# A transform and two gated layers on one core: another order at the transform's beginning, and a second engine for the copies of high halves

## The chip, the cores and the metric

The kernel runs on one core of one Trainium2 chip. The metric is device time in microseconds (us), lower is better: 1006.93 us is the median of three runs of the kernel before (1006.16 to 1008.03).

TensorE (PE) multiplies, VectorE (DVE), ScalarE (ACT) and GpSimd (POOL) do the elementwise work, and SyncE (SP) issues most DMAs. ScalarE issues a few DMAs at the start, and GpSimd issues one in each step of the first layer. Each engine works through its own list of instructions in order and waits on semaphores for the others.

## The reference

```python
def _attn_ref(x):                      # x: (2, 3008, 256)
    X = np.fft.fft(x, axis=1)
    X = np.fft.fft(X, axis=2)
    return X.real.astype(np.float32)
def _moe_ref(x, w_gate, w_val, w_out): # x: (6016, 256), 256 -> 1536 -> 256
    gate = 1.0 / (1.0 + np.exp(-(x @ w_gate)))
    val = x @ w_val
    return (gate * val @ w_out).astype(np.float32)
def _moe2_ref(x, w_in, w_out):         # 256 -> 2048 -> 256
    h = x @ w_in
    g = h * np.cos(h)
    return (g @ w_out).astype(np.float32)
def reference(**kwargs):
    ...
    x = attn_out.reshape(B * S, D)
    x = _moe_ref(x=x, **moe_kwargs)
    return _moe2_ref(x=x, **moe2_kwargs)
```

The weights reach the chip as float64 numbers (the kernel reads their bits), x as float32. The kernel computes in float32.

## The kernel before

**Transform.** A sequence of 3008 = 64 x 47 is transformed in three stages of matmuls. In the first, 16 chunks (c = 0 to 15) of 8 columns each are multiplied with the 47-point table: the columns of x are the stationary operand, and each chunk fills two banks of PSUM (the tile `ps`), which ScalarE or VectorE copies to the tile `D1`. x comes in 256 KB pieces: `load_x2` (line 421) fetches two chunks with three DMAs into one of three buffers `raws`, in turn. Chunks 0 and 1 lie in `raws[0]` and have DMAs of their own; `raws[1]` holds chunks 2 and 3, `raws[2]` chunks 4 and 5, then `raws[0]` again 6 and 7, and so on. A buffer is loaded anew when TensorE has left it. The loads write 96 of 128 partitions, so each buffer is zeroed once before its first load. Behind chunk `CX0` four small matmuls on the tile `xs` (line 476) make a correction that ScalarE and VectorE add to `D1`. The second stage (`stage_b`, table `T1`) has 12 groups, the third (`stage_c` and `c_piece`, table `T3`) 6 blocks of tokens; it leaves the tokens' even and odd parts in `eo`. Part of the third stage is done between the first steps of the next layer.

**First layer.** 72 steps s, each one tile of 128 of the 1536 hidden units f for one of six blocks of 502 token pairs t (table `TF`; the first 12 steps take f = 0 to 5 for t = 0 and 1, the next 12 take f = 6 to 11). In a step TensorE makes two pairs of products (`ab(s, 0)` into banks 4 and 5, `ab(s, 1)` into banks 6 and 7). VectorE joins them (`even`, lines 645 to 647, then `tokens`, line 653). ScalarE takes the sigmoid (line 815), GpSimd multiplies gate and value (`times`, line 657), ScalarE splits the product into a high part and a negated one (`hi1`, lines 755 and 756), and GpSimd issues a DMA that adds the product to the latter (`lo1`, line 693), which leaves the low part. Four steps later TensorE multiplies with the output weights (`out1(s - 4)`, lines 670 to 673). All matmuls are done on split values: high times high, low times high, high times low. The second layer has the same form with a cosine and starts when the first has ended.

**Weights.** They arrive as float64 bits, and the chip turns them into float32. A unit of 128 x 512 numbers goes through `dec_steps`: scale (ScalarE, line 170), sign (line 145 or 146), size (line 151 or 153), clamp (VectorE, line 157), shift (VectorE, line 162), add (GpSimd, line 167); for the first layer's input weights a difference and a sum (lines 231 and 232); and then the split, `hilo_steps`: a copy to the high half and a subtraction for the low one.

```python
        def high():
            at[:] = views()
            A.copy(at[0], src())
        ...
        return [(A, .63, high), (VG, {V: 1.1, G: 1.3}, low)]
```

A unit stands in a slot `u0` to `u17`: the input weights of tile f in `u0` to `u11`, the output weights of tiles 2k and 2k + 1 in the slot numbered 12 + k. So `u15` holds the output weights of tiles 6 and 7, and `out1(12)`, the first product of tile 6, needs it in step 16.

**What sets the order.** The engines' lists are fixed when the program is built. A planner keeps a clock for each engine (`clk`), adds estimated times to them, and puts steps of the weights' decoding between the regular work wherever an engine's clock leaves room (`fill`, line 318); `may` (line 256) says which engine takes a step that two can do, and `need` (line 352) finishes a unit at the place where it is first used. While the transform runs, the low half goes to whichever of VectorE and GpSimd would end it first; once the first layer has begun (`begun`) all low halves go to GpSimd. Small changes of the estimates or of the order of loads move many instructions. The constants `cmax`, `czero` and `cone`, which the decoding on VectorE reads, lie at the end of PSUM bank 7, the bank of the second product of `ab(s, 1)`.

**The beginning**, lines 427 to 447:

```python
        for r in raws[1:]:
            G.memset(r, 0.0)
        ...
        A.dma_start(out=xs[0:96], in_=x0)
        clk[DQ] = 4.3
        for p in range(1, NX2):
            load_x2(p)
            if p == 1:
                fill(DQ, clk[DQ] + 1.7)
```

Of the kernel before, what the change touches and what calls it, by code (L numbers as in the profile page):

```python
# [34 lines left out]
JC = 8  # L35
# [1 line left out]
JH = 3  # L37
NX2 = 3
NWARM = 7
CX0 = 4  # L40
L1, L2 = 4, 5

INV2PI = float(np.float32(1 / (2 * np.pi)))
# [12 lines left out]
def fft_moe_moe(ctx: ExitStack, tc: tile.TileContext, x, x0, head, w1, w1s, wo1, w2, t1, t3, out):  # L56
# [19 lines left out]
    ps = pp.tile([128, 8, 512], F32, name="ps")  # L76
# [47 lines left out]

    DQ = nc.sync
    clk = {V: 0.0, A: 0.0, G: 0.0, DQ: 0.0}
    VG, VA = (V, G), (A, V)
    begun = [False]

    def spend(e, us, after=0.0):  # L130
# [47 lines left out]
    def hilo_steps(views, src):  # L178
        at = []

        def high():
            at[:] = views()
            A.copy(at[0], src())

        def low(e):
            e.tensor_tensor(out=at[1], in0=src(), in1=f32(at[0]), op=ALU.subtract)

        return [(A, .63, high), (VG, {V: 1.1, G: 1.3}, low)]

    ws = [dpool.tile([128, 2 * UC], F32, name=f"ws{u}") for u in range(NF2)]  # L190

# [59 lines left out]
    beside = [0.0]  # L251

    def cost(step, e):
        return (step[1][e] if step[0] in (VG, VA) else step[1]) + (beside[0] if e is V else 0)

    def may(un, e):

        step = un[2][0]
        if step[0] not in (VG, VA):
            return e is step[0]  # L260
        if e not in step[0] or begun[0] and step[0] is VG and e is V:
            return False
        if begun[0] and step[0] is VG:
            return True
        other = step[0][1 - step[0].index(e)]
        mine, theirs = (max(un[3], clk[q]) + step[1][q] for q in (e, other))
        return mine <= theirs + (VLATE if e is V else 0)
# [6 lines left out]
    def step_of(un, e=None):  # L274
        if len(un[2][0]) > 3 and not un[1]:
            at = max(un[3], clk[un[2][0][0]])
            while not (room_at(at, True) or free):
                finish(next(o for o in live if o[1] and o[0][0] in DIRECT))
            bf = room_at(at) or room_at(at, True) or free[0]
            free.remove(bf)  # L280
            un[1].append(bf)
            un[4].append(bf[0])
            un[3] = max(un[3], bf[2])
        step = un[2].pop(0)
        if step[0] in (VG, VA):
            e = e or (G if begun[0] and step[0] is VG else min(step[0], key=lambda q: max(clk[q], un[3]) + step[1][q]))
            step[2](e)
        else:
            e = step[0]
            step[2]()  # L290
        un[3] = spend(e, cost(step, e), un[3]) + (3.3 if e is DQ else .15)
        if not un[2]:
            live.remove(un)
            free.extend([buf, end, un[3], of] for buf, end, _, of in un[1])
# [23 lines left out]
    def fill(e, until):  # L318

        while True:  # L320
            begin(until)
            for un in live:
                step = un[2][0]
                if may(un, e):
                    at = max(un[3], clk[e])
                    if len(step) > 3 and not un[1] and not room_at(at):
                        continue
                    if at + cost(step, e) <= until:
                        step_of(un, e)
                        break  # L330
            else:
                if e is DQ and clk[e] + 1.5 <= until:
                    if queued:
                        load_next()
                        continue
                    if len(todo) > held[0] and todo[0][0] == "w2":
                        ready = [p for p in pairs() if max(bf[2] for bf in p) <= until]
                        if ready:
                            start(ready[0])
                            continue  # L340
                return
# [69 lines left out]
    with tc.tile_pool(name="xp", bufs=1) as xp:  # L411

        raws = [xp.tile([128, 2 * JC, 2, 64], F32, name=f"raw{i}") for i in range(NX2)]

        def rows(e, out, src):
            for k in range(3):
                e.dma_start(out=out[k:128:4], in_=src[32 * k:32 * (k + 1)])

        def load_x2(p):

            raw, src = raws[p % NX2].rearrange("p (c j) s n -> p c j s n", c=2), x[:, 2 * p:2 * p + 2]
            rows(DQ, raw, src)
            spend(DQ, 2.2)

        DQ.dma_start(out=hd[0:96], in_=head)
        DQ.dma_start(out=raws[0][0:96, JH:JC], in_=x[:, 0, JH:JC])
        DQ.dma_start(out=raws[0][0:96, JC:2 * JC], in_=x[:, 1])
        G.memset(warm, 0.0)  # L430
        for c_, k_ in ((cmax, FMAX), (czero, 0.0), (ps[:, 7, 509:510], 1.0)):
            V.memset(c_, k_)
        V.memset(hd2, 0.0)
        V.memset(hd[96:128], 0.0)
        V.memset(raws[0][96:128], 0.0)
        V.memset(raws[0][0:96, 0:JH], 0.0)
        for r in raws[1:]:
            G.memset(r, 0.0)
        V.memset(xs[96:128], 0.0)
        V.memset(halfpi, HALFPI)  # L440
        rows(A, hd2, head[:, 0:96])
        A.dma_start(out=xs[0:96], in_=x0)
        clk[DQ] = 4.3
        for p in range(1, NX2):
            load_x2(p)
            if p == 1:
                fill(DQ, clk[DQ] + 1.7)


        for _ in range(NWARM):  # L450
            PE.matmul(ps[:, 6, 0:128], warm, warm, start=True, stop=True)

        now = 3.5
        clk[V] = clk[G] = clk[A] = 4.5
        for c in range(NJC):
            if c == 10:
                DQ.dma_start(out=T1, in_=t1)
                DQ.dma_start(out=T3, in_=t3)
                spend(DQ, 1.4)
            ahead_a = AHA if c < NJC - 2 else (4, .4, 2, .5) if c < NJC - 1 else (4, .1, 2, -.8)  # L460
            nx = (c + 1) // 2 - 1 + NX2
            if nx < NJC // 2:

                ahead_a = (6.9 + (2 * nx - 1) * 1.79 + XLATE - 2.3 - 2.2 - now - 1.79,) + ahead_a[1:]
            slot(now, 1.79, ahead_a)
            b0 = 2 * (c % 3)
            for j in range(JC):
                q = ps[:, b0 + j // 4, (j % 4) * 96:(j % 4 + 1) * 96]
                if c == 0 and j < JH:
                    xj = hd[:, 96 + j * 128:96 + (j + 1) * 128]  # L470
                else:
                    xj = raws[c // 2 % NX2][:, c % 2 * JC + j].rearrange("p s n -> p (s n)")
                PE.matmul(q, xj, T2[c // 2 > 0], start=True, stop=True)  # L473
            if c == CX0:
                for i in range(2):
                    PE.matmul(ps[:, b0 + i, 384:480], xs[:, i], T2[0], start=True, stop=True)
            if c % 2 and c // 2 + NX2 < NJC // 2:
                clk[DQ] = max(clk[DQ], now + 1.79)
                load_x2(c // 2 + NX2)

            def evac(c=c, b0=b0, at=now + (1.79 if c else 3.4)):
                src = ps[:, b0:b0 + 2, 0:384].rearrange("p a (q c) -> p c a q", c=96)
                dst = D1[:, :, c * JC:(c + 1) * JC].rearrange("p c (a q) -> p c a q", a=2)
                if c < NJC - 1 and max(clk[V], at) + .4 < max(clk[A], at):
                    regular(V, .96, at)
                    V.tensor_copy(dst, src)
                elif c < NJC - 1:
                    regular(A, .8, at)
                    A.copy(dst, src)
                else:  # L490
                    regular(V, .5, at - .85)
                    V.tensor_copy(dst[:, :, 0], src[:, :, 0])
                    regular(A, .4, at)
                    A.copy(dst[:, :, 1], src[:, :, 1])
                if c == CX0:

                    A.mul(half, ps[:, b0, 384:480].rearrange("p (b s k) -> p b s k", b=B, s=2), .5)
                    f128 = ps[:, b0 + 1, 384:480].rearrange("p (b s k) -> p b s k", b=B, s=2)  # L500
                    d = D1[:, :, 0].rearrange("p (b s k) -> p b s k", b=B, s=2)
                    for r, sg in ((slice(0, 64), .5), (slice(64, 128), -.5)):
                        for cs in range(2):
                            V.scalar_tensor_tensor(
                                out=d[r, :, cs], in0=f128[r, :, 1 - cs], scalar=(sg if cs else -sg),
                                in1=half[r, :, cs], op0=ALU.mult, op1=ALU.add)
                    spend(A, .2)
                    spend(V, .5, clk[A])

            after.append(evac)  # L510
            now += 1.79 if c else 3.4
# [454 lines left out]
```

## Time and profile before

| | |
|---|---|
| median of three runs | 1006.93 us |
| the profiled execution: its time, its span | 1007.07 us, 1004.9 us |
| TensorE busy | 991.4 us (99%) |
| ScalarE, VectorE, GpSimd busy | 795.0, 747.4, 653.2 us |
| granted TensorE clock, mean | 0.999 |
| DMA rate in the first two of 40 slices of the span (50 us) | 302 and 332 GB/s |

The span runs from the first to the last instruction; the rest of an execution's time lies around it. TensorE is busy nearly all the time, so a stretch in which it waits is what the others can add or save. The profile counts the 99% over all stages: the first 36 us are the transform's first stage, the second and third end near 70 us, the first layer's steps run to about 480 us, and the second layer takes the rest.

### The profile page before, as it was taken

What the parts mean: (1) busy time and instruction counts of PE and PEld (TensorE: products, weight loads), DVE (VectorE), ACT (ScalarE), POOL (GpSimd) and SP (SyncE); (2) the same over time, 40 slices, a digit from 0 to 9 for tenths busy, and PEclk for the clock granted to TensorE, in tenths of its full rate; (3) what the DMA queues carried; (4) which work ended last, traced back from release to release, by engine and by line L of the source; (5) the groups of instructions that cost most, each with busy time, mean ns of one, the idle gap of its engine ahead of it and who ended that gap; (6) DMA issues with size and microseconds to landing.
All of it is one profiled execution on the core that took longest, in us unless ns stands there. A gap on an engine that the chain in (4) does not pass through costs nothing.

```text
span 1004.9 us, 13355 instructions
## 1 busy us (share of the span) xinstructions
PE 991.4 (99%) x4570; PEld 826.3 (82%) x4570; DVE 747.4 (74%) x1018; ACT 795.0 (79%) x1231; POOL 653.2 (65%) x521
## 2 busy tenths in 40 slices
PE   9999999999999999998999999999999999999998
PEld 8997888878888888787888888888888888888886
DVE  4898977887778777775777677777777777776775
ACT  5798767777777786856888888888988888888886
POOL 2678998888889898784445464554645455464643
PEclk9999999999999999999999999999999999999999
DMA  8804566678768768899000000000000000000000
GB/s 302 332 1 83 98 104 128 126 151 179 153 133 168 170 151 181 214 245 226 1 1 21 21 1 21 1 22 13 8 22 1 21 1 21 21 0 22 1 21 21
DMA packets 34644, 85.59 MB, mean 85 GB/s; under 512 B 3312, under 2 KB 25136, under 8 KB 33904
## 3 DMA queue, kind: packets, MB, share of 16 engines
q0 software_dynamic: 19584, 37.02, 21.4%
q1 hardware_dynamic: 14736, 47.59, 13.3%
q8 instruction: 36, 0.59, 0.3%
q14 instruction: 32, 0.26, 0.1%
q10 hardware_dynamic: 256, 0.14, 0.1%
HBM read 33.16 MB, written 14.56 MB: 47 GB/s over the span
## 4 chain that ended last, share of the span: by engine, by line
PE 90%; DMA 3%; DVE 3%; ACT 2%; issue 1%; POOL 1%; DVEq 0%; ACTq 0%; POOLq 0%; SPq 0%
PE ps L722 26%; PE ps L627 14%; PE ps L628 14%; PE ps L629 14%; PE ps L670 5%; PE ps L672 5%; PE ps L673 5%; PE ps L473 3%; DVE D L653 2%; DMA D<-D 2%; PE ps L569 1%; PE ps L529 1%; PE ps L530 1%; POOL D L657 1%; DMA ws<-D 1%
## 5 line engine op out<-in xcount | busy, mean ns | idle before, releaser
L748 POOL TENSOR_TENSOR D<-D,D 128x502 fp32r<-128x502 f32 x191 | 248.9, 1303 | 253.4 <-ACT D L747 239.1
L722 PE MATMUL ps<-D,u 128*128 128x502 f32 x1152 | 291.7, 389 | 0.0
L627 PE MATMUL ps<-es,u 128*128 128x502 f32 x672 | 262.9, 391 | 2.1 <-DVE D L653 1.2
L628 PE MATMUL ps<-es,u 128*128 128x502 f32 x672 | 262.3, 390 | 0.0
L629 PE MATMUL ps<-es,u 128*128 128x502 f32 x672 | 261.6, 389 | 0.0
L722 PEld LDWEIGHTS ps<-D,u 128*128 128x128 f32 x1152 | 216.7, 188 | 45.1
L657 POOL TENSOR_TENSOR D<-D 128x502 f32<-128x502 f32 x144 | 198.6, 1522 | 46.4 <-ACT D L815 46.1
L733 DVE SCALAR_TENSOR_TENSOR D<-D,ps 128x502 f32<-128x502 int32 x192 | 130.1, 678 | 122.0 <-POOL D L748 102.5
L653 DVE TENSOR_TENSOR D<-D,ps 128x1004 f32<-128x1004 f32 x144 | 172.9, 1201 | 49.5 <-PE ps L629 22.4
L732 ACT ACTIVATE D<-ps 128x502 int32<-128x502 f32 x192 | 113.1, 589 | 60.7 <-PE ps L629 58.1
L815 ACT ACTIVATE D<-D 128x1004 f32<-128x1004 f32 x72 | 75.0, 1041 | 97.1 <-DVE D L653 97.1
L627 PEld LDWEIGHTS ps<-es,u 128*128 128x128 f32 x672 | 126.5, 188 | 30.7 <-DVE D L653 2.3
L628 PEld LDWEIGHTS ps<-es,u 128*128 128x128 f32 x672 | 126.9, 189 | 25.9
L629 PEld LDWEIGHTS ps<-es,u 128*128 128x128 f32 x672 | 126.4, 188 | 26.4
L734 DVE SCALAR_TENSOR_TENSOR D<-D 128x502 f32<-128x502 int32 x192 | 142.3, 741 | 6.6
L740 DVE TENSOR_TENSOR D<-D,ps 128x502 f32<-128x502 f32 x192 | 128.8, 671 | 17.1 <-ACT D L739 17.1
L645 DVE SCALAR_TENSOR_TENSOR D<-eo,w,ps 128x502 f32<-128x502 f32 x144 | 101.4, 735 | 32.3 <-PE ps L629 31.9
L739 ACT ACTIVATE D<-D 128x502 f32<-128x502 f32 x192 | 120.0, 625 | 6.1
L738 ACT ACTIVATE D<-D 128x502 f32<-128x502 f32 x192 | 118.7, 618 | 4.3 <-DVE D L734 2.8
L747 ACT CAST D<-D 128x502 fp32r<-128x502 f32 x192 | 114.5, 596 | 0.3 <-DVE D L740 0.3
L672 PE MATMUL ps<-D,u 128*128 128x502 f32 x288 | 112.5, 391 | 1.2 <-ACT eo L689 1.2
L673 PE MATMUL ps<-D,u 128*128 128x502 f32 x288 | 111.9, 389 | 0.0
(95 smaller groups left out, 1103.8 us busy)
## 6 DMA issues: line engine op xcount, KB each, us to landing
D<-D POOLq DMA_DIRECT2D x72, 502.0 KB, 5.8
D<-in_w_dram SPq DMA_DIRECT2D x16, 512.0 KB, 4.9
ws<-D SPq DMA_DIRECT2D x16, 512.0 KB, 3.8
u<-ws SPq DMA_DIRECT2D x16, 512.0 KB, 5.4
u<-in_w_dram SPq DMA_DIRECT2D x12, 512.0 KB, 7.9
out_dram<-D SPq DMA_DIRECT2D x24, 251.0 KB, 2.7
raw<-in_x_dram SPq DMA_DIRECT2D x21, 256.0 KB, 5.1
u<-in_wo_dram SPq DMA_DIRECT2D x6, 512.0 KB, 7.7
```

Of the source, the lines that this page charges most:

```text
L627: PE.matmul(o, w_hi, m_hi, start=first, stop=False)
L628: PE.matmul(o, w_lo, m_hi, start=False, stop=False)
L629: PE.matmul(o, w_hi, m_lo, start=False, stop=last)
L653: V.tensor_tensor(out=gv[s][:, :, c:c + PC], in0=sas, in1=ps[:, 6:8, 0:PC], op=op)
L657: G.tensor_tensor(out=gv[p][:, 1, m], in0=gv[p][:, 1, m], in1=gv[p][:, 0, m], op=ALU.mult)
L672: PE.matmul(o, WO1(f)[:, 0, m], h[:, 0, sg], start=first, stop=False)
L673: PE.matmul(o, WO1(f)[:, 1, m], h[:, 0, sg], start=False, stop=False)
L722: PE.matmul(o, WO2(f)[:, i, d * 128:(d + 1) * 128], h[:, m], start=(f == 0 and i == m == 0), stop=(f == NF2 - 1 and m == 1))
L733: V.scalar_tensor_tensor(out=r, in0=k, scalar=-C1, in1=h, op0=ALU.mult, op1=ALU.add)
L734: V.scalar_tensor_tensor(out=r, in0=k, scalar=-C2, in1=r, op0=ALU.mult, op1=ALU.add)
L740: V.tensor_tensor(out=r, in0=r, in1=ps[:, 4 + s % 4, 0:PC], op=ALU.mult)
L748: (V if s == N2S - 1 else G).tensor_tensor(out=h[:, 1], in0=r, in1=f32(h[:, 0]), op=ALU.subtract)
```

## The change

The second buffer of x is zeroed in two halves, by GpSimd and VectorE, and it is the first thing VectorE does. The constants in PSUM come later. The load of `raws[2]` is issued right behind that of `raws[1]`, and the first weights (`fill(DQ, ...)`) follow both. The correction from `xs` moves from chunk 4 to chunk 6, and `xs`'s own DMA stands behind the loads in the text (ScalarE still issues it fourth). The copies to high halves may be taken by ScalarE or GpSimd during the transform; afterwards ScalarE has all of them, as before.

```diff
-CX0 = 4
+CX0 = 6
...
-        def high():
+        def high(e):
             at[:] = views()
-            A.copy(at[0], src())
+            if e is A:
+                A.copy(at[0], src())
+            else:
+                G.tensor_copy(at[0], src())
...
-        return [(A, .63, high), (VG, {V: 1.1, G: 1.3}, low)]
+        return [(AG, {A: .63, G: .8}, high), (VG, {V: 1.1, G: 1.3}, low)]
...
-        if e not in step[0] or begun[0] and step[0] is VG and e is V:
+        if e not in step[0]:
             return False
-        if begun[0] and step[0] is VG:
-            return True
+        if begun[0] and step[0] is not VA:
+            return e is (G if step[0] is VG else A)
...
-        for c_, k_ in ((cmax, FMAX), (czero, 0.0), (ps[:, 7, 509:510], 1.0)):
-            V.memset(c_, k_)
+        for e in (G, V):
+            r = raws[1].rearrange("p j s n -> p (j s n)")
+            e.memset(r[:, 0:JC * 128] if e is G else r[:, JC * 128:], 0.0)
         V.memset(hd2, 0.0)
         V.memset(hd[96:128], 0.0)
         V.memset(raws[0][96:128], 0.0)
         V.memset(raws[0][0:96, 0:JH], 0.0)
-        for r in raws[1:]:
+        for c_, k_ in ((cmax, FMAX), (czero, 0.0), (ps[:, 7, 509:510], 1.0)):
+            V.memset(c_, k_)
+        for r in raws[2:]:
             G.memset(r, 0.0)
...
-        A.dma_start(out=xs[0:96], in_=x0)
         clk[DQ] = 4.3
         for p in range(1, NX2):
             load_x2(p)
-            if p == 1:
-                fill(DQ, clk[DQ] + 1.7)
+        A.dma_start(out=xs[0:96], in_=x0)
+        fill(DQ, clk[DQ] + 1.7)
```

The changed program's line numbers are three to five higher (line 186 is 189, line 657 is 662).

SyncE's list at the beginning, before and then now (`raw1` and `raw2` are the buffers of x, `u0` and `u1` the first input weights, `eo0` here the room for the weights' odd row):

```order
L419 DMA raw1_115<-in_x_dram 32x2048 x3
L195 DMA eo0_82<-in_w1s_dram 128x48
L195 DMA u0_0_64<-in_w1_dram 128x1024
L419 DMA raw2_116<-in_x_dram 32x2048 x3
L195 DMA u1_0_65<-in_w1_dram 128x1024
```

```order
L422 DMA raw1_115<-in_x_dram 32x2048 x3
L422 DMA raw2_116<-in_x_dram 32x2048 x3
L198 DMA eo0_82<-in_w1s_dram 128x48
L198 DMA u0_0_64<-in_w1_dram 128x1024
L198 DMA u1_0_65<-in_w1_dram 128x1024
```

The second load of x now stands ahead of the first weights, and everything behind the fifth row is in the same order.

GpSimd's list in the first layer, from the product `times(11)` to `times(16)` before, then from `times(14)` to `times(16)` now (`D1` is the room for products and decoding, L657 or L662 is `times`, L693 or L698 the DMA of `lo1`, L186 or L189 a low half):

```order
L657 TENSOR_TENSOR D1_90<-D1_90 128x502 x2
L693 DMA D2_376<-D1_90 128x2x502
L186 TENSOR_TENSOR u11_1_1151<-D1_90,u11_1_1151 128x4x128
L186 TENSOR_TENSOR u15_1_1153<-D1_90,u15_1_1153 128x2x256
L657 TENSOR_TENSOR D1_90<-D1_90 128x502 x2
L693 DMA D2_376<-D1_90 128x2x502
L657 TENSOR_TENSOR D1_90<-D1_90 128x502 x2
L693 DMA D2_376<-D1_90 128x2x502
L167 TENSOR_TENSOR D1_90<-D1_90,u16_0_80 128x512
L167 TENSOR_TENSOR D1_90<-D1_90,u17_1_818 128x512
L657 TENSOR_TENSOR D1_90<-D1_90 128x502 x2
```

```order
L662 TENSOR_TENSOR D1_90<-D1_90 128x502 x2
L698 DMA D2_372<-D1_90 128x2x502
L167 TENSOR_TENSOR D1_90<-D1_90,u15_0_79 128x512
L167 TENSOR_TENSOR D1_90<-D1_90,u16_0_80 128x512
L662 TENSOR_TENSOR D1_90<-D1_90 128x502 x2
L698 DMA D2_372<-D1_90 128x2x502
L189 TENSOR_TENSOR u15_1_1295<-D1_90,u15_1_1295 128x2x256
L189 TENSOR_TENSOR u16_1_1297<-D1_90,u16_1_1297 128x2x256
L662 TENSOR_TENSOR D1_90<-D1_90 128x502 x2
```

The low half of `u15` stood behind `times(11)` and `lo1(10)`; it now stands behind `times(15)` and `lo1(14)`. The first rows of the two pieces are `times(11)` and `times(14)`.

VectorE's list between `tokens(4)` (first row) and `even(5)` (last row), before and then now (`u8`, `u9`, `u10` are units in decoding):

```order
L653 TENSOR_TENSOR D1_90<-D1_90,ps_63 128x2x502 x2
L162 SCALAR_TENSOR_TENSOR D1_90<-D1_90,ps_63 128x512
L157 SCALAR_TENSOR_TENSOR D1_90<-u10_0_74,ps_63 128x512
L645 SCALAR_TENSOR_TENSOR D1_90<-eo0_82,w128_88,ps_63 128x502 x2
L653 TENSOR_TENSOR D1_90<-D1_90,ps_63 128x2x502 x2
```

```order
L658 TENSOR_TENSOR D1_90<-D1_90,ps_63 128x2x502 x2
L157 SCALAR_TENSOR_TENSOR D1_90<-u8_0_72,ps_63 128x512
L162 SCALAR_TENSOR_TENSOR D1_90<-D1_90,ps_63 128x512
L157 SCALAR_TENSOR_TENSOR D1_90<-u9_0_73,ps_63 128x512
L650 SCALAR_TENSOR_TENSOR D1_90<-eo0_82,w128_88,ps_63 128x502 x2
```

Three steps of decoding stand there in place of two.

## Rows read from the trace of the kernel before

**Rows 1.** The page, busy time of each engine.
```profile
PE 991.4 (99%) x4570; PEld 826.3 (82%) x4570; DVE 747.4 (74%) x1018; ACT 795.0 (79%) x1231; POOL 653.2 (65%) x521
```

**Rows 2.** Waits of TensorE from 160 us on: us in total, times, longest.
```profile
PE ps L670 <- DMA D<-D: 2.5, 1, 2.5
PE ps L672 <- ACT eo L689: 1.2, 1, 1.2
PE ps L627 <- DVE D L157: 0.7, 1, 0.7
```

**Rows 3.** Timeline of TensorE, 1 to 16 us: start, us, what [idle before].
```profile
1.00 3.36 PE L451 MATMUL ps<-early 128*128 128x128 f32 x14 [1.00 <-POOL early L430]
4.15 1.43 PE L473 MATMUL ps<-early 128*128 128x96 f32 x6
5.38 3.46 PE L473 MATMUL ps<-early,raw 128*128 128x96 f32 x26
9.45 3.78 PE L473 MATMUL ps<-early,raw 128*128 128x96 f32 x32 [0.62 <-issue]
14.11 2.00 PE L473 MATMUL ps<-early,raw 128*128 128x96 f32 x16 [0.88 <-ACT D L489]
```

**Rows 4.** Timeline of SyncE's DMA queue, 0 to 20 us.
```profile
2.72 2.68 SPq L419 DMA_DIRECT2D raw<-in_x_dram  x3
...
6.70 2.15 SPq L419 DMA_DIRECT2D raw<-in_x_dram  x3
...
9.59 1.74 SPq L419 DMA_DIRECT2D raw<-in_x_dram  x3
...
13.27 1.75 SPq L419 DMA_DIRECT2D raw<-in_x_dram  x3
```

**Rows 5.** DMA issues, 9.5:11.36 and 13.2:15.1: KB each, median us to landing.
```profile
raw<-in_x_dram SPq DMA_DIRECT2D x3, 256.0 KB, 6.3
...
raw<-in_x_dram SPq DMA_DIRECT2D x3, 256.0 KB, 6.6
```

**Rows 6.** Timeline of GpSimd and of VectorE, 0 to 9 us, two memsets.
```profile
0.88 3.55 POOL L438 MEMSET raw<- 128x2048 f32 x2
...
4.19 0.38 DVE L436 MEMSET raw<- 96x384 f32 x1
```

**Rows 7.** Timelines of ScalarE, VectorE and TensorE, steps 1 and 5.
```profile
77.66 0.62 ACT L183 CAST u<-D 128x512 fp32r<-128x512 f32 x1
...
92.28 2.43 DVE L653 TENSOR_TENSOR D<-D,ps 128x1004 f32<-128x1004 f32 x2 [1.88 <-DMA D<-D]
94.63 0.68 DVE L162 SCALAR_TENSOR_TENSOR D<-D,ps 128x512 uint32<-128x512 uint32 x1
95.23 0.68 DVE L157 SCALAR_TENSOR_TENSOR D<-u,ps 128x512 f32<-128x512 f32 x1
...
95.96 0.49 PE L627 MATMUL ps<-es,u 128*128 128x502 f32 x1 [0.24 <-DVE D L157]
```

**Rows 8.** Timelines of ScalarE, GpSimd and TensorE, steps 15 and 16.
```profile
157.87 1.06 ACT L756 ACTIVATE D<-D 128x1004 fp32r<-128x1004 f32 x1
...
152.62 1.69 POOL L693 DMA_DIRECT2D D<-D  x1
153.39 3.49 POOL L186 TENSOR_TENSOR u<-D,u 128x512 fp32r<-128x512 f32 x2
...
159.47 1.20 POOL L693 DMA_DIRECT2D D<-D  x1
...
157.05 0.39 PE L673 MATMUL ps<-D,u 128*128 128x502 f32 x1
```

**Rows 9.** Windows: stretch, busy of PE, PEld, DVE, ACT, POOL, granted clock, DMA.
```profile
469.70:472.20 2.50, 0.00 (x0) 0.00 (x0) 0.30 (x1) 2.47 (x4) 1.20 (x1) 1.00 1.10 274
...
1000.00:1002.80 2.80, 0.29 (x2) 0.00 (x0) 0.00 (x0) 0.82 (x2) 0.00 (x0) 1.00 0.50 184
1002.90:1004.90 2.00, 0.00 (x0) 0.00 (x0) 0.00 (x0) 0.00 (x0) 0.00 (x0) 0.50 0.00 0
```

More of the change, by code (lines that the diff above doesn't have):

```diff
@@ L126, in fft_moe_moe @@
     clk = {V: 0.0, A: 0.0, G: 0.0, DQ: 0.0}
-    VG, VA = (V, G), (A, V)
+    VG, VA, AG = (V, G), (A, V), (A, G)
     begun = [False]
@@ L253, in cost @@
     def cost(step, e):
-        return (step[1][e] if step[0] in (VG, VA) else step[1]) + (beside[0] if e is V else 0)
+        return (step[1][e] if type(step[0]) is tuple else step[1]) + (beside[0] if e is V else 0)
     def may(un, e):
         step = un[2][0]
-        if step[0] not in (VG, VA):
+        if type(step[0]) is not tuple:
             return e is step[0]
-        if e not in step[0] or begun[0] and step[0] is VG and e is V:
+        if e not in step[0]:
             return False
-        if begun[0] and step[0] is VG:
-            return True
+        if begun[0] and step[0] is not VA:
+            return e is (G if step[0] is VG else A)
         other = step[0][1 - step[0].index(e)]
@@ L284, in step_of @@
         step = un[2].pop(0)
-        if step[0] in (VG, VA):
-            e = e or (G if begun[0] and step[0] is VG else min(step[0], key=lambda q: max(clk[q], un[3]) + step[1][q]))
+        if type(step[0]) is tuple:
+            e = e or ((G if step[0] is VG else A) if begun[0] and step[0] is not VA else min(step[0], key=lambda q: max(clk[q], un[3]) + step[1][q]))
             step[2](e)
```

## The prediction

> **What bounds the kernel now.** I read the busy times first: TensorE works 99% of the span [rows 1], so the other engines count only where TensorE waits. Its waits come next. From 160 us on there are three, 4.4 us together [rows 2]; each belongs to one place in the program (the end of a block of tokens, the last steps of the first layer) and not to an engine that is behind everywhere. At the beginning two chunks of the first stage start late, by 0.62 and 0.88 us [rows 3]; they are the first chunks of `raws[1]` and `raws[2]`, so they wait for x. Near 95 us TensorE waits 0.24 us for VectorE's decoding [rows 7]. Then I put the three lists of the changed program beside these times, and asked of each moved step who waits for it.
>
> **The beginning.** The change lets `raws[2]` arrive ahead of the first weights and lets the load of `raws[1]` start when two half memsets are done, rather than one whole. A whole one takes 1.8 us and ends at 2.7, where the load starts [rows 4, 6]; two halves side by side end near 1.8, and the load then starts at about 2.1, when SyncE is through with the ones ahead. VectorE pays with about 0.9 us ahead of its other memsets, and drops the three small ones behind them; its last memset of `raws[0]` ended at 4.57 [rows 6] and would end near 5.2, and TensorE's first matmul on that buffer began at 5.38 [rows 3]. What little this delays falls into the 0.62 us that follow.
>
> The two waits are an upper bound of the gain: 1.50 us. The lower bound is nothing: the same bytes still have to come ahead of the later loads. The load for chunks 8 and 9 bears that out. Its three DMAs are issued from 13.27 on, the last at about 14.4, and take 6.6 us to land [rows 4, 5]: 21.0 us. It stands behind the same weights as before. Chunk 8 began at about 14.11 + 2.00 + 3 x 1.89 = 21.8 us [rows 3], so it can move up by 0.8 us at most unless that landing moves too. The load for chunks 6 and 7 (last issue about 10.75, 6.3 us [rows 4, 5], landing near 17.0) says nearly the same. I take -0.8 us. Moving the four matmuls on `xs` two chunks down costs nothing: they take the same time there, and what they wait for is long there. Giving some high copies to GpSimd costs nothing by itself either: GpSimd idles for long stretches until the first layer begins. A copy on GpSimd stands nowhere in the trace; its bounds are half a memset of 2048 numbers over 1024, so 0.45 us for 512, and half of what two low halves of 512 took, 1.75 us [rows 6, 8], and either is hidden there.
>
> The stages behind pass the gain on. By the lists, ScalarE and VectorE have some two instructions less each between the last chunk and the first step, since later weights' decoding has moved into the first layer. That is also the price.
>
> **VectorE between `tokens(4)` and `even(5)`.** Three decoding steps stand there in place of two. The second product of `ab(5, 1)` goes to bank 7 and waited for the last of them: it ended at 95.91 and TensorE went on at 95.96, 0.24 us late [rows 7]. One step more is 95.23 - 94.63 = 0.60 us [rows 7], straight on TensorE's path. There is a second small term: one high copy (0.62 us [rows 7]) now stands between ScalarE's last evacuation and its first sigmoid, none before. If it delays `hi1(0)` and so the DMA that `tokens(4)` waited for (1.88 us [rows 7]), up to 0.4 us more appear at the same place. I take +0.8 us, from 0.6 to 1.0.
>
> **The low half of `u15`.** This is the large term. `out1(12)` in step 16 is the first to use it, and its second matmul, the first that multiplies with the low half, ran at 157.05 without waiting [rows 8]: the half was made four steps of `times` earlier. In the changed list it stands behind `times(15)` and behind the DMA of `lo1(14)`, both in GpSimd's order. That DMA instruction began at 159.47, because `hi1(14)` on ScalarE ended at 157.87 + 1.06 = 158.93 [rows 8]. So TensorE arrives before GpSimd can even begin. How long a low half takes behind such a DMA is in the rows of `lo1(13)`, which had two low halves behind it: the DMA instruction from 152.62 to 154.31, the halves from 153.39, both done at 156.88, so 1.28 us each after 154.31, and the first done 2.97 us after the DMA began [rows 8]. The same behind `lo1(14)` gives 159.47 + 2.97 = 162.44, a wait of 5.4 us. With the shorter DMA instruction that `lo1(14)` had (1.20 us) it is 159.47 + 1.20 + 1.28 = 161.95, 4.9 us; if a low half weren't held up by the DMA instruction at all (start 0.77 us behind it), 161.52 and 4.5 us. I take +5.2 us. The term doesn't depend on the beginning, since sigmoid, `hi1` and `times` of these steps follow TensorE's own products: when TensorE comes earlier, so do they. Behind `u15` the halves of `u16` and `u17` have two steps or more to spare, and from step 22 on the lists are the same.
>
> **TensorE's clock.** In that wait TensorE does one matmul (it needs only the high half, a copy behind `hi1(14)`) and otherwise stands still for 5 us. The granted clock stayed at its full level (2.4 GHz) through 2.5 us without a matmul near 470 us, and stood at the half level (1.2 GHz, 0.50) 2.6 us after the last matmul, at 1000.29 [rows 9]. A stall twice as long lies beyond both. What a fall costs is bounded from the start: matmuls ran from 1.00 us, and passes of 96 columns took 1.43 / 6 = 238 ns until 5.6 us, 3.46 / 26 = 133 ns then, and 3.78 / 32 = 118 ns from 9.45 on [rows 3]. The loss was half of 4.6 us and 26 x 15 ns, so 2.7 us. The other bound is 0, a clock that stays. I take +1.5 us, a little above the middle, since the end of the span shows a fall after a shorter pause.
>
> The Trainium skill (TensorE: Matmul & The Clock Gate, "What's actually happening") puts it as a rule: the half rate is the default, and activity alone releases the full one. By the rule the stall ends at the half rate and 1013.6 us comes out; by the row near 470 us alone the clock would stay, 1012.1 us. The end of the span agrees with the rule; no run here shows a five-microsecond pause with one matmul in it.
>
> **The sum.** 1007.07 - 0.8 + 0.8 + 5.2 + 1.5 = 1013.8 us for the profiled execution, whose span of 1004.9 us and 2.2 us around it are both in it; the median lies 0.14 us below that execution, so 1013.6 us.
>
> **The rivals.**
> 1. The clock stays up in the stall. For it: the row near 470 us. The sum without the 1.5 us: 1012.1 us.
> 2. GpSimd falls behind as well. In steps 11 to 13 it has an addition, a difference and a low half more than before, some 2.7 us (1.28 and two shorter ones). If the products of `times` then come late for `lo1` and TensorE waits for that too, it is 1016.3 us. Against it: two other steps move out of the same stretch.
> 3. Not slower: the stall is paid back. TensorE's three later waits are 4.4 us [rows 2]; if the other engines, which gain 5 us on TensorE in the stall, were merely behind there, these waits would go, and with the clock up 1012.1 - 4.4 = 1007.7 us is no change. It decides from the point where an engine carries a lag from step to step. Against it: in those steps VectorE and ScalarE wait for TensorE too, so they carry none, and each wait comes out of the steps right before it.
> 4. The change doesn't show: the low half of `u15` comes in time, the gain at the beginning and the loss at step 5 cancel, and 1012.1 - 5.2 = 1006.9 us remains. It would need the half 5 us earlier than its place in GpSimd's list allows.
>
> **How the numbers follow.** The forecast has 0.54, rival 1 0.31, rival 2 0.07, rival 3 0.04, rival 4 0.04. About 0.2%, 2.0 us, is what a measurement of this kernel can tell from no change. Rivals 3 and 4 lie within it, so same is 0.07 and faster 0.01 (a gain of 1.5 us at the beginning and no price at step 5 don't reach 2.0 us together, but some unseen wait may go), slower 0.92. The low end: 1.5 us gained, 0.6 at step 5, a stall of 4.5 us and no fall of the clock give 1010.5 us. The high end: nothing gained, 1.0, 5.4 and 2.7 us give 1016.0 us. I give 1010.4 to 1015.8 us.
>
> **What would show it.** In the profile after, the first chunks of `raws[1]` and `raws[2]` start with a wait of less than 0.62 and 0.88 us, and the second stage starts some 0.8 us earlier. Near 95 us one wait of TensorE for VectorE grows to about 0.8 us. In step 16 TensorE waits about 5 us at line 678 for GpSimd's line 189, the largest wait of the page, and the matmuls behind it take twice as long for a while if the clock fell. The prediction is wrong if no wait for GpSimd stands there, if the wait is under 4 us, or if TensorE's three later waits [rows 2] shrink by as much.

## The result, and the profile after

The changed kernel takes 1018.08 us (median of 4 runs, 1017.54 to 1018.92), the kernel before on the same chip 1007.48 us: a ratio of 1.0109, 95% interval 1.0091 to 1.0126. It is slower, as forecast, but by 10.6 us and not by 6.7, and 1018.08 lies above the range that was given (1010.4 to 1015.8). The profiled execution took 1018.13 us with a span of 1016.3 us.

First the page's busy times, and then the waits of TensorE from 160 us on (us in total, times, longest); they answer to [rows 1, 2].

```profile
PE 997.3 (98%) x4570; PEld 831.3 (82%) x4570; DVE 745.8 (73%) x1016; ACT 794.4 (78%) x1229; POOL 654.8 (64%) x526
```

```profile
PE ps L675 <- DMA D<-D: 2.5, 1, 2.5
PE ps L677 <- ACT u L184: 2.4, 1, 2.4
PE ps L678 <- POOL u L189: 2.0, 1, 2.0
PE ps L632 <- DVE D L157: 0.7, 1, 0.7
```

TensorE is busy 6 us longer with the same 4570 matmuls: the windows below show the clock at half its level for some of that time. Two of the waits are new, 2.4 and 2.0 us. They and the longer busy time do not yet make 11 us; the rest is at the beginning. The timeline of TensorE there (start, us, what, idle before) answers to [rows 3]:

```profile
4.85 3.14 PE L478 MATMUL ps<-early,raw 128*128 128x96 f32 x26
8.71 7.36 PE L478 MATMUL ps<-early,raw 128*128 128x96 f32 x64 [0.72 <-DMA raw<-in_x_dram]
18.83 3.49 PE L478 MATMUL ps<-early,raw 128*128 128x96 f32 x15 [2.76 <-DMA raw<-in_x_dram]
```

The chunks of `raws[1]` start at 8.71 (9.45 before), and those of `raws[2]` follow without a wait. So TensorE is through chunk 5 at 16.07 us, 2.1 us ahead, and then has no data: chunk 6 starts 2.76 us later. Its first 15 matmuls take 3.49 us where 16 took 2.00. Windows of the same stretch, of the stretch behind the stall in step 16, and of one near 483 us (busy time of PE, PEld, DVE, ACT, POOL, then the granted clock, the DMA share and GB/s):

```profile
16.00:18.00 2.00, 0.07 (x1) 0.00 (x0) 1.31 (x2) 1.33 (x3) 0.23 (x1) 0.97 0.98 381
18.00:20.00 2.00, 1.17 (x6) 1.20 (x6) 1.64 (x3) 1.57 (x4) 0.14 (x1) 0.50 1.01 418
20.00:22.00 2.00, 2.00 (x11) 2.00 (x11) 0.96 (x1) 0.66 (x1) 1.89 (x2) 0.50 1.03 420
...
165.80:168.00 2.20, 2.20 (x5) 1.78 (x6) 0.00 (x0) 0.00 (x0) 2.20 (x3) 0.50 1.05 173
482.60:485.00 2.40, 2.40 (x6) 1.97 (x7) 0.68 (x1) 0.52 (x1) 0.00 (x0) 0.50 1.13 209
```

The clock fell to its half level three times. To see what each place costs, I set the start of the same matmul in one trace against its start in the other; the difference grows only where time is lost:

| matmul | before, us | after, us | difference |
|---|---|---|---|
| chunk 6, first | 18.18 | 18.83 | +0.65 |
| second stage, first | 36.77 | 40.73 | +3.96 |
| step 5, ahead of the wait | 94.77 | 98.30 | +3.53 |
| step 5, behind it | 95.96 | 99.85 | +3.89 |
| `out1(12)`, first | 156.83 | 163.24 | +6.41 |
| `out1(12)`, second | 157.05 | 165.76 | +8.71 |
| step 17, first product | 159.98 | 171.36 | +11.38 |
| end of the block near 421 us | 421.21 | 431.63 | +10.42 |
| behind the DMA wait near 472 us | 473.69 | 485.21 | +11.52 |
| end of the last matmul | 1000.29 | 1011.97 | +11.68 |

So 3.5 us are lost at the beginning (3.96 at the second stage, of which 0.4 come back before step 5), 0.4 in step 5, 4.8 in the stall of step 16 and 2.7 in the half clock behind it. Later the wait of 1.16 us near 421 goes, and a fall of the clock near 482 takes as much again.

Step 16 itself, on ScalarE, GpSimd and TensorE; this answers to [rows 8]:

```profile
161.62 1.06 ACT L761 ACTIVATE D<-D 128x1004 fp32r<-128x1004 f32 x1
162.56 1.15 ACT L184 CAST u<-D 128x512 fp32r<-128x512 f32 x2
...
163.21 1.20 POOL L698 DMA_DIRECT2D D<-D  x1 [1.01 <-issue]
163.99 2.94 POOL L189 TENSOR_TENSOR u<-D,u 128x512 fp32r<-128x512 f32 x2
...
163.24 0.50 PE L677 MATMUL ps<-D,u 128*128 128x502 f32 x1 [2.40 <-ACT u L184]
165.76 0.79 PE L678 MATMUL ps<-D,u 128*128 128x502 f32 x1 [2.02 <-POOL u L189]
```

Read down: `hi1(14)` ends on ScalarE at 162.68, then the high copy of `u15` and of `u16` are made, and TensorE's first matmul of `out1(12)` follows the first of them at 163.24. `lo1(14)` starts on GpSimd at 163.21, its two low halves behind it, and the first ends where L678 starts, 2.55 us after the DMA instruction began.

Step 5, on VectorE and TensorE, answers to [rows 7]: three decoding steps, and the wait is 0.71 us where it was 0.24.

```profile
97.79 0.68 DVE L157 SCALAR_TENSOR_TENSOR D<-u,ps 128x512 f32<-128x512 f32 x1
98.51 0.69 DVE L162 SCALAR_TENSOR_TENSOR D<-D,ps 128x512 uint32<-128x512 uint32 x1
99.11 0.68 DVE L157 SCALAR_TENSOR_TENSOR D<-u,ps 128x512 f32<-128x512 f32 x1
...
99.85 0.49 PE L632 MATMUL ps<-es,u 128*128 128x502 f32 x1 [0.71 <-DVE D L157]
```

What is left to explain is why chunk 6 has no data. SyncE's queue, what it waited for up to 12 us (us in total, times, longest), and the landing of the load for chunks 6 and 7 (issues from 9.6 to 12.7 us, median us to landing); the queue and the landing answer to [rows 4, 5]:

```profile
2.20 5.74 SPq L422 DMA_DIRECT2D raw<-in_x_dram  x6
...
9.62 3.06 SPq L422 DMA_DIRECT2D raw<-in_x_dram  x3
```

```profile
SPq L422 <- DMA early<-in_head_dram: 2.1, 2, 1.5
```

```profile
raw<-in_x_dram SPq DMA_DIRECT2D x3, 256.0 KB, 7.8
```

SyncE issues the loads of `raws[1]` and `raws[2]` one behind the other, but stops for 1.5 us between them, at 4.6 us: it waits until a load of the head has landed. In the trace both loads count on the same semaphore, so the later one cannot be issued before the earlier one is done. The three loads of the head are issued by ScalarE as soon as VectorE has zeroed `hd2`; that is 2.08 us now (1.33 before), since VectorE zeroes its half of `raws[1]` first. The last DMA for chunk 6 is issued at 11.00 and lands at 18.69 us, where 17.06 was the figure before.

### The profile page after: what moved, and what is told of

It is laid out like the page before. It is cut to its first block, busy times and chain, and to the rows that moved or that the text cites. A ratio compares the mean times of both kernels' runs of the same rounds, so it can differ in the third digit from the quotient of the medians.

```text
span 1016.3 us, 13358 instructions
## 1 busy us (share of the span) xinstructions
PE 997.3 (98%) x4570; PEld 831.3 (82%) x4570; DVE 745.8 (73%) x1016; ACT 794.4 (78%) x1229; POOL 654.8 (64%) x526
## 4 chain that ended last, share of the span: by engine, by line
PE 88%; DVE 3%; ACT 3%; DMA 3%; issue 1%; POOL 1%; SPq 0%; ACTq 0%; DVEq 0%; POOLq 0%
PE ps L727 26%; PE ps L632 14%; PE ps L633 14%; PE ps L634 14%; PE ps L675 6%; PE ps L678 5%; PE ps L677 5%; DVE D L658 2%; PE ps L478 2%; DMA D<-D 2%; PE ps L574 1%; PE ps L534 1%; PE ps L535 1%; DMA raw<-in_x_dram 1%; ACT D L761 1%
## 5 line engine op out<-in xcount | busy, mean ns | idle before, releaser
L662 POOL TENSOR_TENSOR D<-D 128x502 f32<-128x502 f32 x144 | 198.6, 1523 | 44.3 <-ACT D L820 44.0
L678 PE MATMUL ps<-D,u 128*128 128x502 f32 x288 | 113.0, 392 | 2.0 <-POOL u L189 2.0
```

Of the source, the lines that this page charges most:

```text
L662: G.tensor_tensor(out=gv[p][:, 1, m], in0=gv[p][:, 1, m], in1=gv[p][:, 0, m], op=ALU.mult)
L678: PE.matmul(o, WO1(f)[:, 1, m], h[:, 0, sg], start=False, stop=False)
```

## The experiments

Two theories stood for the late load. A: the head's loads are late, so is the load into `raws[2]`, and the DMA engines run short of work from 6 to 12 us. B: the two weights of 512 KB that stand ahead of the load for chunk 6 now go out together, at 8.70 and 9.09 us, where the first of them went out at 6.23 us, ahead of the load of `raws[2]`. For step 16 the theory was the place of `u15`, against an engine that is late whatever the order. The runs of one group shared the runs of the kernel before, whose median differed a little from group to group (1008.5, 1008.0 and 1009.1 us), so ratios are to be compared, and traces.

**1. The decoding of every `wo1` weight two steps earlier (e1_need2).**
```
-            need(("wo1", TF[s - L1][1] // 2))
+            need(("wo1", TF[min(s - L1 + 2, N1S - 1)][1] // 2))
```


> The changed kernel, with the decoding of each wo1 weight finished two steps ahead of its first use instead of in that step (the low half of u15 then stands behind times(13), not behind times(15)). Theory (the stall in step 16 is the place of that half in GpSimd's order, and the clock falls in it): the two waits of 2.40 and 2.02 us near 160 to 166 us go, the granted clock stays at 1.00 there, and 4.4 + 2.7 = 7.1 us are saved: about 1011.0 us. Rival (GpSimd and ScalarE are behind there whatever the order): the wait moves to ab(17) or to u16, at most 2 us are saved, 1016 us or more.

1016.36 us, ratio 1.0079 (1.0051 to 1.0107). The two waits of step 16 are gone, as the theory had it, but the time came back at other places, and the rival's number is the one that was met. VectorE and TensorE near 192 us:

```profile
189.69 2.37 DVE L690 SCALAR_TENSOR_TENSOR eo<-ps,eo 128x502 f32<-128x502 f32 x3
191.98 0.68 DVE L162 SCALAR_TENSOR_TENSOR D<-D,ps 128x512 uint32<-128x512 uint32 x1
192.58 1.29 DVE L146 SCALAR_TENSOR_TENSOR D<-D,ps 128x512 uint16<-128x512 uint16 x1
...
193.92 0.77 PE L632 MATMUL ps<-es,u 128*128 128x502 f32 x1 [1.88 <-DVE D L146]
```

The planner moved later decoding steps of VectorE behind the three evacuations at the end of a block of tokens (L690), where VectorE has no time to spare. The clock fell there and again behind a wait of 1.81 us at 230.43. The edit did too much to tell the theories apart.

**2. `hd2` zeroed first (e2_hd2).**
```
+        V.memset(hd2, 0.0)
         for e in (G, V):
...
-        V.memset(hd2, 0.0)
```


> The changed kernel, with VectorE zeroing hd2 before its half of raws[1] and not behind it. Theory A (the three small loads of the head start 0.75 us later than before the change, and the first load into raws[2] waits for one of them to land): the loads of the head start near 1.3 us, the first load into raws[2] near 5.0 and not at 6.19 us, the load for chunk 6 lands near 17.5 instead of 18.69 us, TensorE waits about 1.5 and not 2.76 us for it, the clock stays up, and 1.2 + 2.9 = 4.1 us are saved: about 1014.0 us. Rival B (the two weights ahead of that load set when it lands): it lands at 18.7 us as it did, and the time stays at 1018.1 us.

1014.73 us, ratio 1.0056 (1.0036 to 1.0077). ScalarE's queue, TensorE at chunk 6 and the window around it:

```profile
1.00 1.86 ACTq L422 DMA_DIRECT2D early<-in_head_dram  x3
...
17.05 2.00 PE L478 MATMUL ps<-early,raw 128*128 128x96 f32 x16 [0.48 <-DMA raw<-in_x_dram]
```

```profile
18.00:20.00 2.00, 2.00 (x21) 2.00 (x19) 1.33 (x1) 1.17 (x2) 1.79 (x2) 1.00 1.02 422
```

The first load into `raws[2]` went out at 5.60, and the load for chunk 6 landed at 16.91 us. The wait is 0.48 us, the clock stays up, and TensorE reaches the second stage at 36.14 us, 0.6 us ahead of the kernel before. Between 10 and 12 us the share of the DMA engines is 0.87 against 0.74 in the changed kernel. Theory A holds, with more effect than it was given. The landing (issues from 9.05 to 11 us, median us to landing):

```profile
raw<-in_x_dram SPq DMA_DIRECT2D x3, 256.0 KB, 6.6
```

Only the place of one memset differs from the changed kernel, and both weights still stand ahead of this load, as they did before the change. So the late `hd2` is what made it late, and rival B falls. The other traces agree: in run 6, with the same remedy, the load landed at 17.20 us; in runs 1, 4, 5 and 7, without one, between 18.50 and 18.93, in run 9 at 17.78.

**3. One weight less in front (e3_one_weight).**
```
         fill(DQ, clk[DQ] + 1.7)
+        held_q, clk[DQ] = clk[DQ], 99.0
...
-                clk[DQ] = max(clk[DQ], now + 1.79)
+                clk[DQ] = max(held_q if c == 1 else clk[DQ], now + 1.79)
```


> The changed kernel, with the second weight behind the load for chunks 6 and 7, not ahead of it. Rival B (the weights in front set when the load for chunk 6 lands): it lands 1.2 us earlier, the transfer time of 512 KB, near 17.5 us; TensorE waits about 1.4 us instead of 2.76, the clock stays up, about 1014.0 us. Theory A alone (the idle stretches of the DMA engines between 6 and 12 us, from the late start of the load into raws[2], set it): it lands less than 0.6 us earlier, TensorE still waits over 2 us, the clock still falls, and the time stays above 1017 us.

1013.49 us, ratio 1.0053 (1.0036 to 1.0071). The load for chunk 6 landed at 16.47 us, chunk 6 waited 0.68 us and chunk 8 0.32, and the clock stayed up. So B's remedy works as well as A's, and by 1.0 us more than was forecast. That does not bear out B as the cause, since run 2 brings the load in time with both weights ahead of it: taking 512 KB from the front makes up for a delay that comes from the head.

**4. and 9. Matmuls to keep TensorE busy (e4_warm, e9_warm12).**
```
+            for _ in range(24 if c == 6 else 0):
+                PE.matmul(ps[:, 6, 0:128], warm, warm, start=True, stop=True)
```


> The changed kernel, with 24 matmuls of 128 columns on a zeroed tile put ahead of chunk 6; their result is not used. Theory (of the loss at the beginning 2.9 us are the clock, which falls because TensorE stands still for 2.76 us): chunk 6 starts at 18.8 us as it did, but the granted clock stays at 1.00 from 16 to 26 us, and 2.9 us are saved: about 1015.2 us. Rival (chunks 6 and 7 run slowly for another reason, or the clock falls whatever TensorE does there): the matmuls of chunk 6 take twice as long as before, 1018.1 us.

1015.34 us, ratio 1.0068 (1.0048 to 1.0089). Each of them ran as two passes, 48 in 5.55 us, so they ended at 21.5 us, long after the load had landed (18.57), and ate up what the clock gave: TensorE reached the second stage at 40.50 us, 3.7 us behind the kernel before. So the time came out as forecast, but not by the forecast way: what this execution gained on the changed kernel came later, where the half clock behind step 16 cost 1.7 us and not 2.7, and the pause for a DMA near 479 us took 0.81 us and not 2.5. With 12:

> The changed kernel with 12 matmuls instead of 24 ahead of chunk 6; each ran as two passes of 0.115 us, so 24 took 5.5 us where 2.8 us were to be filled. Theory (the fall of the clock ahead of chunk 6 is 2.9 us of the loss): the matmuls end when the load for chunk 6 lands, near 18.8 us, the clock stays at 1.00, TensorE is about 0.7 us behind the kernel before at 40 us instead of 4.0, and the span of the profiled execution is 3 us shorter than that of the changed kernel: about 1015 us. Rival (the matmuls only trade one delay for another): 1018 us, with TensorE 3 us or more behind at 40 us.

1014.18 us, ratio 1.0054 (1.0037 to 1.0071). TensorE's timeline and a window of this run:

```profile
16.42 2.87 PE L473 MATMUL ps<-early 128*128 128x128 f32 x24
19.12 1.92 PE L480 MATMUL ps<-early,raw 128*128 128x96 f32 x16
```

```profile
18.00:20.00 2.00, 2.00 (x21) 2.00 (x19) 1.67 (x2) 0.89 (x2) 1.35 (x2) 1.00 1.02 420
```

Chunk 6 starts later than in the changed kernel, 19.12, and runs at full speed: TensorE reaches the second stage 1.4 us behind the kernel before (38.14 against 36.77 us), not 4.0. From chunk 6 to the second stage it took 38.14 - 19.12 = 19.02 us, and 40.73 - 18.83 = 21.90 us in the changed kernel: of the loss of 3.96 us at that place the clock is 2.9. In this execution the load itself landed earlier, at 17.78 us; but run 4, where it landed at 18.57, kept the clock as well.

**5. and 6. `u15` alone moved (e5_u15), and with `hd2` first (e6_u15_hd2).**
```
             need(("wo1", TF[s - L1][1] // 2))
+            if s == 14:
+                keep = dict(clk)
+                need(("wo1", 3))
+                clk.update(keep)
```


> The changed kernel, with only the last steps of u15 (wo1[3]) moved: its high and low half are made in step 14, the low half behind times(13) as one of two; VectorE's order is that of the changed kernel, word for word. Theory (the place of u15 in ScalarE's and GpSimd's order is the whole of the stall in step 16; what the first try, which also moved later weights, lost near 192 and 228 us came from VectorE's decoding behind a block's end): the waits of 2.40 and 2.02 us in step 16 go, the granted clock stays at 1.00 there, no new wait comes at 192, and 4.4 + 2.7 = 7.1 us are saved: about 1011.0 us. Rival (ScalarE and GpSimd are late there whatever the order, and the wait only moves): 2 us or less saved, 1016 us or more.

1009.77 us, ratio 1.0012 (0.9996 to 1.0028). TensorE's only wait between 100 and 225 us, and its window in step 16:

```profile
PE ps L632 <- DVE D L157: 1.0, 1, 1.0
```

```profile
160.00:166.00 6.00, 6.00 (x29) 4.97 (x28) 4.17 (x5) 5.41 (x8) 6.00 (x7) 1.00 0.49 86
```

The stall and the fall of the clock behind it are gone, and up to 222 us nothing has come in their place (the difference to the kernel before stays between 4.0 and 4.3 us from 100 us on). Against the changed kernel's 1.0109 the ratio is 9.8 us lower; the two traces show 7.5 of it in step 16, and the rest lies within the two intervals. The place of `u15` is the cause of that stall.

> The changed kernel, with u15 moved as in the run before and VectorE zeroing hd2 before its half of raws[1]. Theory (the two stalls are separate and are all that the change loses): chunk 6 waits about 0.5 us as it did with hd2 alone, the stall in step 16 is gone, TensorE is 0.6 us ahead of the kernel before at 20 us and no more than 0.5 us behind it at 222 us: about 1007.3 us, no difference from the kernel before. Rival (the early lead is bought with a weight that comes late in the first layer): the time stays over 1010 us.

1007.78 us, ratio 0.9992 (0.9978 to 1.0006): as forecast, no difference from the kernel before. TensorE's waits from 100 us on:

```profile
PE ps L675 <- DMA D<-D: 2.7, 1, 2.7
PE ps L677 <- ACT eo L694: 2.5, 1, 2.5
PE ps L632 <- DVE D L157: 0.7, 1, 0.7
```

The two stalls are separate, and they are all that the change loses, as far as the interval can tell. In this trace TensorE is 0.2 us ahead of the kernel before at 222 us and 1.4 behind at the end, because the wait near 422 us is 2.5 us and not 1.2. The high copies on GpSimd are still in this kernel, so by themselves they cost nothing that this can tell.

**7. and 8. The two parts of the change apart (e7_begin_only, e8_copies_only).** In the first the function `high` and the choice of engine are those of the kernel before, in the second the beginning and `CX0 = 4` are.

> The kernel before, with the changed beginning alone (zeroing, order of loads, the products of xs two chunks later); all high copies stay on ScalarE. Theory (the beginning loses by itself, and the late u15 comes only of both parts together, through the planner): TensorE waits some 2.8 us ahead of chunk 6 and the clock falls there, 3.6 us lost at 40 us; the low half of u15 stands behind times(14) here and comes in time, so no wait over 1 us in step 16: about 1011.0 us. Rival (the stall in step 16 belongs to the beginning): 1017 us or more.

> The kernel before, with the choice of engine for high copies alone (ScalarE or GpSimd); the beginning is as it was. Theory: no wait of 2.8 us ahead of chunk 6; the low half of u15 stands behind times(14) and comes in time; the time is that of the kernel before within 1 us, about 1007.5 us. Rival (the copies on GpSimd themselves cost time, or they alone make u15 late): 1011 us or more, with waits in step 16.

1024.21 us, ratio 1.0157 (1.0137 to 1.0177), and 1026.54 us, ratio 1.0167 (1.0138 to 1.0196): both expectations fell. The beginning behaves as I thought: with it alone chunk 6 waits 2.05 us (2.8 forecast) and TensorE is 2.6 us late at the second stage (3.6 forecast); without it TensorE is level with the kernel before at 20 us. But the stall in step 16 is in both, and longer. TensorE's and ScalarE's waits with the copies alone, from 150 us on and in step 16:

```profile
PE ps L675 <- ACT u L184: 6.0, 2, 5.4
PE ps L676 <- POOL u L189: 2.7, 2, 2.1
...
ACT u L184 <- POOL D L235: 2.1, 1, 2.1
ACT u L184 <- POOL D L167: 1.1, 1, 1.1
```

Here the high copy itself is 5.4 us late: ScalarE waits for GpSimd's addition of `u15` (L167), which stands behind `lo1(14)` there, with GpSimd idle for 1.0 us ahead of that DMA. The wait for the sum (L235) comes after this copy and holds another one. TensorE's wait of 2.1 us for a low half (L676) comes two steps later, for the next unit. I had looked at the place of the low half in GpSimd's list only, not at the steps ahead of it. So the late `u15` belongs to neither part alone: three different shifts of the plan made it late, and the order of the kernel before is one in which it came in time. That other shifts would do the same is a guess.

**10. The three remedies together (e10_u15_hd2_one).** The edits of 2, 3 and 5 in one kernel.

> The kernel with u15 moved and hd2 zeroed first, and the second weight behind the load for chunks 6 and 7 as well: the three remedies together. Theory: chunk 6 waits less than 0.3 us, TensorE is about 1.0 us ahead of the kernel before at 20 us (0.35 us without the third remedy), no stall in step 16, and with the 0.3 us lost in step 5 some 0.6 us remain: 1007.2 us against 1008.0 us of the kernel before, at the bound of what can be told. Rival (the load for chunks 8 and 9 comes late in its turn, behind two weights): no gain over the run with two remedies.

1007.17 us against 1009.05, ratio 0.9985 (0.9975 to 0.9994): 1.5 us less than the kernel before by the ratio, with an interval that ends just below 1. From the run with two remedies (0.9992) it cannot be told apart. TensorE's timeline, chunk 7 and the first matmuls of chunk 8:

```profile
18.16 1.95 PE L479 MATMUL ps<-early,raw 128*128 128x96 f32 x16
20.92 1.33 PE L479 MATMUL ps<-early,raw 128*128 128x96 f32 x10 [0.81 <-DMA raw<-in_x_dram]
```

Chunk 6 has no wait, and at chunk 7 TensorE is 1.8 us ahead (19.96 before); then chunk 8 waits 0.81 us for its load, which lands at 20.79 (20.99 before), as the rival had it, and a lead of 0.8 us is left. That is the bound which the prediction drew from that load.

## Why the prediction was wrong

**The beginning is the step that failed.** It said: "The load for chunks 6 and 7 [...] landing near 17.0) says nearly the same. I take -0.8 us." Measured are +3.5 us, and the range had no room for a loss there: its high end has "nothing gained". The premise that failed is that the landing stays where it was. The load landed at 18.69 us, 1.6 us later, while TensorE came 2.1 us earlier; so TensorE stood still for 2.76 us, and the clock fell in that wait. The prediction priced such a fall for step 16 and not here, and of the 3.96 us lost at the second stage it is 2.9 (run 9). I had seen that VectorE's memsets move ("VectorE pays with about 0.9 us"), and followed that to TensorE's first matmul, but not to `hd2`, ScalarE's loads of the head behind it, and the load into `raws[2]` that waits for one of these to land. Run 2 shows what the term would have been with the premise: with `hd2` first the load lands at 16.91 us, chunk 6 waits 0.48 us, the clock stays up, and the second stage starts 0.6 us early, near the 0.8 us of the forecast. Its sum of gains was sound; the list of what hangs on a memset was not complete. The price of a copy on GpSimd was bounded rightly, between 0.45 and 1.75 us: the five in the changed kernel, all before 56 us, took 0.61 us (median).

**VectorE at step 5** (+0.8, from 0.6 to 1.0) was right in place and too large: one more decoding step cost 0.47 us in the wait and 0.36 in the difference of the two traces. In runs 2, 3, 5 and 10, which have the same three steps, the difference is 0.7 us, within the range; so its size changes from one execution or beginning to another. The second, smaller term of that step isn't seen.

**The low half of `u15`** (+5.2, from 4.5 to 5.4) was right in mechanism and nearly in size: 4.8 us. The working had the high copy behind `hi1(14)` and one matmul in the stall, but the sign that it gave (about 5 us at line 678, the largest wait of the page) put all of it on the low half. There are two waits: 2.40 us for the high copy and 2.02 us for the low half, and the largest wait is the one ahead of chunk 6. The low half was done 2.55 us behind the start of `lo1(14)`'s DMA instruction, between the bounds of 2.05 and 2.97 us that were drawn for it; GpSimd was idle for 1.01 us ahead of that instruction, so it was not behind. That the stall can be taken out by itself is shown by run 5.

**The clock behind it** (+1.5, from 0 to 2.7) cost 2.7 us in this trace, the upper bound. That it met the bound is luck: behind the same stall it cost 1.7 us in runs 2 and 4, 2.7 in run 3 and 2.3 in run 9. The bound was read from the durations of the first matmuls; the granted clock of the windows from 1 to 6 us reads 1.00 in the kernel before, so that stretch alone did not show that its slow matmuls were a fall of the clock. Here the granted clock is 0.50 from 165.8 to 168 us, and also from 18 us on, behind the other stall. The Trainium skill (TensorE: Matmul & The Clock Gate, "What's actually happening") has the throttled clock as the default, which activity releases. Both stalls agree with it.

**The rivals.** Rival 1 (the clock stays up) is refuted by the 0.50. Rival 2 (GpSimd behind as well) has no part: GpSimd was idle ahead of `lo1(14)` in the changed kernel and in runs 7 and 8, and what made it late there is its order. Rival 3 (paid back) is not shown. The wait near 421 us went, 1.2 us, and as much came back as a fall of the clock near 482 us; but that wait is also gone in run 10, which has no stall in step 16, and is 2.2 us in run 2, which has it. Rival 4 (`u15` comes in time) is refuted by the two waits. With the beginning at +3.5 instead of -0.8 and the clock at 2.7, the prediction's own sum would have been 1007.07 + 3.5 + 0.4 + 4.8 + 2.7 = 1018.5 us, against 1018.13 measured. The parts come from the same trace, so this only says that no large part is missing.

What stays open: how much the beginning loses from one execution to another (3.96 us at the second stage here, but 3.0, 2.7 and 2.6 in runs 1, 5 and 7, which begin the same way), and why one of three equal loads at times lands 2 us behind the two issued with it (18.93 against 16.82 in run 1).

## What to carry to other kernels

When a load is moved up, ask two things: what else is issued behind the instruction that was put in front (here a memset of 0.91 us was put ahead of one of 0.14 us, on which three small loads hung, on one of which the next large load hung), and what the engine that now comes early will do while it waits. Here TensorE came 2.1 us early to chunk 6 and was 3.96 us late at the second stage, since its clock fell in the wait; in run 2, with a wait of 0.48 us and no fall, it kept 0.6 us. Where a planner sets the order, list for each late operand where all of its steps stand, the addition and the high copy as well as the low half, and compare with the step that first uses it.

## What the runs showed of the hardware

The pause near 472 to 492 us, in which TensorE waits for a DMA, is much the same in 11 of the profiles, 2.3 to 2.9 us long, and the clock fell behind it in five of them and not in the other six: in the changed kernel after 2.54 us (0.50, the last row of the windows further up), in the kernel before not after 2.55, and with 12 matmuls ahead of chunk 6 not after 2.59:

```profile
476.80:479.30 2.50, 0.00 (x0) 0.00 (x0) 0.27 (x1) 2.47 (x4) 1.20 (x1) 1.00 1.09 274
479.40:482.00 2.60, 2.60 (x12) 2.17 (x13) 0.68 (x1) 0.56 (x2) 0.00 (x0) 1.00 1.13 209
```

It also fell behind a wait of 1.81 us in run 1 (230.43 us), and stayed up behind the pause of 2.90 us in run 10. So the length of a pause of this size does not decide it, and 1.1 us more or less in one execution says nothing of the kernel. The row of the kernel before on which I weighed the clock [rows 9] was one of two that this pause can give.
